# A gated scan and two feed-forward blocks: decay tiles of 129 columns per pair of heads, and three more chunks transposed by TensorE

## The chip, the cores and the metric

One Trainium2 chip, one of its cores. The metric is the device time of one execution in microseconds (us), smaller is better. Before the change the median of three executions is 585.96 us (584.48 to 587.40).

## What is computed

The reference has three stages. The first is a recurrence over time with a decay per key channel:

```
state = zeros((B, H, D, D))                       # B=4, H=8, S=768, D=48, fp32
for t in range(S):
    state = alpha[:, :, t, :, None] * state + einsum('bhd,bhe->bhde', k[:, :, t], v[:, :, t])
    y[:, :, t] = einsum('bhd,bhde->bhe', q[:, :, t], state)
```

`alpha` is drawn from 0.8 to 1.0. The heads of `y` are laid side by side to `x` of 4 x 768 x 384, and two feed-forward blocks follow: one with token mixing (`xk = mu_k*x + (1-mu_k)*x_prev`, `xr` likewise), `relu(xk @ w_k)**2 @ w_v` gated by `sigmoid(xr @ w_r)`; and one with `h = relu(x @ w_in)`, a convolution of three taps in time, a sigmoid gate, and `(h * gate) @ w_out`. The model width is 384, the inner width 1024.

## The kernel before, in words

The recurrence is done in chunks of C = 128 steps: 6 chunks for each of the 4 sequences, 24 in all. Two heads share the 128 partitions of a tile ("a pair"), so four pairs lie side by side in the free dimension. For each chunk three functions run:

- `prep(c)` (line 672) loads alpha, k, q and v, brings alpha, k and q from rows (time on the partitions) to columns (channel on the partitions), and makes the decays. `bt` is a product of the decays that runs backwards from the end of a pair, `gt` one that runs forwards; each is one `tensor_tensor_scan` over all four pairs at once. `kd = k*bt` and `qd = q*gt` are what the matmuls take, and `tt` holds, for each channel, the product over the whole chunk.
- `attend(c)` (line 717) scales the state `ss` by `tt`, forms the scores from `qd` and `kd` within the chunk (masked into `am`), and adds the chunk's keys and values to `ss`.
- `advance(c)` (line 763) makes the chunk's output from `am`, `vt`, `qd` and the kept states `ub`, and writes it into `xt`.

There are 12 units of T = 256 steps. A unit runs `mix` and `split`, `stage_k`, `stage_r`, `stage_v` (first block), `stage_h` and `stage_o` (second block). Products of two fp32 values are made as three matmuls of a high and a low part (`mm`, line 819); in the first two units some weights are still whole fp32 (`early_k`, `wvw`, `wrw`). While a unit runs, the two chunks of the next one are attended and the two after that prepared (`prep(c0 + 2)` in the loop at line 1074, `prep(n + 2)` in `att`, line 1046).

Two ways of transposing exist in `prep`, chosen by `by_pe = c < NPE`, with NPE = 5:

- By TensorE (chunks 0 to 4): rows are loaded with one DMA per tensor (`load(..., rows=True)`, line 651, runs of one head's 48 values), `turned` (line 685) takes a PSUM bank of the pool `banks` (line `turns`, at most two at a time) and transposes the four pairs against `ident`. Alpha is then copied by ScalarE out of PSUM; k and q are read by VectorE from PSUM in the very multiplication that makes `kd` and `qd`.
- By VectorE (chunks 5 to 23): four DMAs per tensor, already spread so that 32x32 block transposes suffice (lines 655 to 660), then one `transpose` (STREAM_TRANSPOSE in the profile) each for alpha, k and q, and the multiplications from SBUF.

The decays themselves, lines 691 to 704 of before:

```
raw = tmp_a.take(pl)                                # alpha lands here, one tile of the five of pool tmps
for x, cs in ((tc_, 0), (v3(adc)[:, :, 1:], slice(1, C))):
    pl.vector.tensor_scalar(x, v3(raw)[:, :, cs], LOW, HIGH, op0=ALU.max, op1=ALU.min)
pl.scalar.activation(raw, raw, AF.Abs, bias=-MID)   # these two count values outside 0.75 .. 1.25
pl.scalar.activation(raw, raw, AF.Relu, bias=-HALF, accum_out=odd[:, c:c + 1])
pl.vector.tensor_tensor_scan(v2(bt)[:, ::-1], ad[:, 1:NP * C + 1][:, ::-1], one_l[:, ::-1], 0.0, ...)
```

So alpha is clipped to 0.75 .. 1.25 in two pieces: the first step of each pair (4 columns) into `tc_`, a tile of `tt`; the other 127 steps of each pair (508 columns) into `ad`, whose first column per pair stays zero and ends the running product there. After the first scan `tc_` is multiplied by `bt`'s first column to give the whole product. If any value was out of range, `step_by_step` computes everything again after the main part; here none is.

`ad`, `bt`, `gt`, `rec_f` and `one_l` exist once; `qd`, `kd`, `tt` and `vt` exist twice; the tiles that take the loaded rows or blocks, `sa`, `sk`, `sq`, exist once (chunks 1 and 2 use spare tiles instead).

The order of the work is set by a planner at build time. All operations are recorded (`note`), each with a modelled cost (`cost`), and `issue` (line 277 of `Plan`) makes a list schedule for the five engines: at each step the engine that can start first takes the ready operation with the longest way to the end (`forward`, `pick`), then the ways are computed again from the end (`backward`); of six rounds the one with the shortest modelled end is written out. Every recorded instruction therefore carries line 297 in the profile, and is told apart by its tiles. A wait on an engine holds up everything behind it in that order. All DMAs go through SyncE's queue; GpSimd does a few memsets and small copies. In the first 30 us of its model the planner fills idle time of TensorE with matmuls that compute nothing (line 1095).

Of the kernel before, what the change touches and what calls it, by code (L numbers as in the profile page):

```python
# [11 lines left out]
F32 = mybir.dt.float32  # L12
# [3 lines left out]
AF = mybir.ActivationFunctionType  # L16
ALU = mybir.AluOpType
# [4 lines left out]
LOW, HIGH = 0.75, 1.25  # L22
MID, HALF = (HIGH + LOW) / 2, (HIGH - LOW) / 2
# [419 lines left out]
def gated_scan_ffn_kernel(  # L443
# [16 lines left out]
    nc = tc.nc  # L460
# [3 lines left out]
    P = 128  # L464
    C = 128
    HC = C // 2
    NP = H // 2
    ND = DM // P
    NF = DFF // P
# [5 lines left out]
    N4 = C // 32  # L475
    NRAW = 2
    NLENT = 12
    NPE = 5
    RAW = 768
    NTMP = 5  # L480
    NTEMP = 3
# [4 lines left out]
    ap = ctx.enter_context(tc.tile_pool(name="ap", bufs=1))  # L486
    fp = ctx.enter_context(tc.tile_pool(name="fp", bufs=1))
    pp = ctx.enter_context(tc.tile_pool(name="pp", bufs=1, space=PSUM))
    pl = Plan(nc)
# [5 lines left out]
    def fill(where, n):  # L495

        where.tile([P, n // 4], F32, name=f"fill{len(fills)}")
        fills.append(n)

    fills = []  # L500
    v3 = lambda x: x.rearrange("p (a b) -> p a b", b=C)
    v2 = lambda x: x.rearrange("p a b -> p (a b)")
    cols = lambda x, n: x.rearrange("p (a b) -> p a b", b=n)

    fill(fp, 160)
    tmps = pool(NTMP, fp, [P, 512], F32, "tmp")
    tmp_a, tmp_f = Line(tmps, 1), Line(tmps, 4)
    raws = Line(pool(NRAW, fp, [P, 2 * RAW], I32, "raw"))
# [12 lines left out]
    ident = cp.tile([P, P], F32, name="ident")  # L521
    mask = cp.tile([P, HC], U8, name="mask")
    mu_ks = cp.tile([P, ND], F32, name="mu_ks")
# [21 lines left out]
    sk = ap.tile([P, NP, N4 * D], F32, name="sk")  # L545
    sa = ap.tile([P, NP, N4 * D], F32, name="sa")
    vt = [ap.tile([P, NP, P], F32, name=f"vt{i}") for i in range(2)]
    ad = ap.tile([P, NP * C + 1], F32, name="ad")
    one_l = ap.tile([P, NP * C], F32, name="one_l")
    rec_f = ap.tile([P, NP * C], F32, name="rec_f")  # L550
    bt = ap.tile([P, NP, C], F32, name="bt")
    gt = ap.tile([P, NP, C], F32, name="gt")
    qd = [ap.tile([P, NP, C], F32, name=f"qd{i}") for i in range(2)]
    kd = [ap.tile([P, NP, C], F32, name=f"kd{i}") for i in range(2)]
    kbt = ap.tile([P, NP, P], F32, name="kbt")
# [106 lines left out]
    def blocks_in(s):  # L662
        return s.rearrange("p a (n d) -> p a n d", n=N4)[:, :, :, 0:32]

    def blocks_out(d):
        return d.rearrange("p a (t n) -> p a n t", n=N4)
# [5 lines left out]
    def prep(c):  # L672
        by_pe = c < NPE
        ia, ik, iq = early[c] if c in early else (sa, sk, sq)
        if c == NPE:

            for x, fill in ((sa, 1.0), (sk, 0.0), (sq, 0.0)):
                for r in (32, 96):
                    pl.gpsimd.memset(x[r:r + 32, :, N4 * D - 32:N4 * D - 16], fill)
        for x, y in ((alpha, ia), (k, ik), (q, iq), (v, vt[c % 2])):  # L680
            load(x, y, c // CPB, (c % CPB) * C, by_pe)
        adc = ad[:, 0:NP * C]
        qc, kc, tc_ = qd[c % 2], kd[c % 2], tt[c % 2]

        def turned(src):
            ps = turns.take(pl)
            for p in range(NP):
                pl.tensor.transpose(ps[:, p * C:(p + 1) * C], v2(src)[:, p * C:(p + 1) * C], ident)
            return ps

        raw = tmp_a.take(pl)
        if by_pe:
            pl.scalar.activation(raw, turned(ia), AF.Copy)
        else:
            pl.vector.transpose(blocks_out(v3(raw)), blocks_in(ia))
        for x, cs in ((tc_, 0), (v3(adc)[:, :, 1:], slice(1, C))):
            pl.vector.tensor_scalar(x, v3(raw)[:, :, cs], LOW, HIGH, op0=ALU.max, op1=ALU.min)
        pl.scalar.activation(raw, raw, AF.Abs, bias=-MID)
        pl.scalar.activation(raw, raw, AF.Relu, bias=-HALF, accum_out=odd[:, c:c + 1])
        pl.vector.tensor_tensor_scan(v2(bt)[:, ::-1], ad[:, 1:NP * C + 1][:, ::-1],  # L700
                                     one_l[:, ::-1], 0.0, op0=ALU.mult, op1=ALU.add)
        pl.vector.reciprocal(v3(rec_f)[:, :, 0], bt[:, :, 0])
        pl.vector.tensor_tensor(tc_, tc_, bt[:, :, 0], op=ALU.mult)
        pl.vector.tensor_tensor_scan(v2(gt), adc, rec_f, 0.0, op0=ALU.mult, op1=ALU.add)
        for x, y, z in ((kc, ik, bt), (qc, iq, gt)):
            if by_pe:
                pl.vector.tensor_tensor(x, v3(turned(y)), z, op=ALU.mult)
                continue
            pl.vector.transpose(blocks_out(x), blocks_in(y))
            pl.vector.tensor_tensor(x, x, z, op=ALU.mult)  # L710
# [290 lines left out]
    with tc.manual_schedule():  # L1001
        nc.vector.memset(ones, 1.0)
        make_identity(nc, ident)
        for y, eng in (((sa, sk, sq), nc.vector), *((x, pl.gpsimd) for x in early.values())):
            for x, fill in zip(y, (1.0, 0.0, 0.0)):
                eng.memset(cols(v2(x), 64)[:, 0:H, D:], fill)
        nc.vector.memset(ad, 0.0)
        nc.vector.memset(odd, 0.0)
        for x in kks.pool.tiles:
            nc.vector.memset(x[:, 0:NP * D], 0.0)  # L1010
        nc.vector.memset(least_s, least)
        nc.scalar.activation(odd1, ones[:, 0:1], AF.Sigmoid)
        for x in vt:
            nc.gpsimd.memset(x[:, :, D:80], 0.0)
        nc.gpsimd.memset(one_l, 0.0)
        nc.gpsimd.memset(v3(one_l)[:, :, C - 1:C], 1.0)
        nc.gpsimd.memset(rec_f, 0.0)
        mf = tmps.tiles[0]
        make_upper_triangular(nc, mf[:, :P])
        for i in range(2):  # L1020
            h = slice(HC * i, HC * i + HC)
            nc.vector.tensor_copy(mask[h], mf[h, h])
        for x in (am, *ub):
            nc.gpsimd.memset(x, 0.0)

        cw_raw = cp.tile([P, 3, NF, 2], I32, name="cw_raw")
        prep(0)
        col = NCH
        lent = Line(Pool([v2(ht)[:, 0:2 * RAW].bitcast(I32)]))
        for x, whole in zip(weights, (None, wrw, wvw, None, None)):  # L1030
            for y in pieces(x[0]):
                i = col - NCH
                weight(*x, y, lent if i < NLENT and i % 3 == 2 else raws, col, whole)
                col += 1
        for r in lent.roots:
            pl.seen.setdefault(ht.tensor.name, []).extend((True, 0, 4, -1, o) for o in r.ops)
        for x, y, z in ((mu_ks, nu_ks, mu_k), (mu_rs, nu_rs, mu_r)):
            pl.sync.dma_start(x, z.rearrange("(a p) -> p a", p=P))
            pl.vector.tensor_scalar(y, x, -1.0, 1.0, op0=ALU.mult, op1=ALU.add)
        for i in range(3):  # L1040
            pl.sync.dma_start(cw_raw[:, i], conv_w[i].bitcast(I32).rearrange("(f p t) -> p f t", p=P, t=2))
        narrow(cw, cw_raw)

        prep(1)

        def att(n):

            attend(n)
            advance(n)
            if n + 2 < NCH:  # L1050
                prep(n + 2)

        def early_k():
            return stage_k(mix(mu_ks, nu_ks, True), True), stage_r(mix(mu_rs, nu_rs, False, True))

        att(0)
        att(1)
        y = early_k()
        att(2)
        att(3)  # L1060
        x0 = stage_v(*y, True)
        y = early_k()
        settle(*weights[1], wrw)
        att(4)
        x1 = stage_v(*y, True)
        settle(*weights[2], wvw)
        big = stage_h(0, x0)
        att(5)
        stage_o(0, big, 0, True)
        xk = mix(mu_ks, nu_ks)  # L1070
        big = stage_h(1, x1)
        xr = mix(mu_rs, nu_rs)
        stage_o(1, big, 0, True)
        for u in range(2, NU):
            c0 = 2 * u + 2
            more = u + 1 < NU
            big = stage_k(xk)
            g = stage_r(xr)
            if more:
                attend(c0)  # L1080
            x = stage_v(big, g)
            if more:
                advance(c0)
                if c0 + 2 < NCH:
                    prep(c0 + 2)
            big = stage_h(u, x)
            if more:
                att(c0 + 1)
                xk = mix(mu_ks, nu_ks)
                xr = mix(mu_rs, nu_rs)  # L1090
            else:
                stage_last(T * NU - 1)
            stage_o(u, big)
        in_range()
        warm = lambda x: nc.tensor.matmul(x[0:64, 0:64], ones, ones, start=True, stop=True)
        pl.issue(600.0, 6, banks.pool, 30e3, warm)

        tc.mark_branch_hint_location("odd", "LikelyTaken", [getattr(mybir.EngineType, e) for e in ("PE", "SP", "DVE", "Activation")])
        n_even = nc.values_load(odd_i, min_val=0, max_val=P)
# [35 lines left out]
```

## Time and profile before

| | |
|---|---|
| median of three executions | 585.96 us |
| the profiled execution: time, span | 586.33 us, 584.4 us |
| its mean granted TensorE clock | 0.981 of full speed |
| busy: TensorE, VectorE, ScalarE, GpSimd | 564.0, 496.4, 434.4, 13.8 us |
| transposes by TensorE (alpha, k, q): sets of four | 15 |
| transposes by VectorE (alpha, k, q) | 57 |

The span runs from the first to the last instruction; the time of the same execution lies 1.9 us above it. PE is TensorE's matmul, PEld its weight load, DVE is VectorE, ACT ScalarE, POOL GpSimd, SP SyncE. A row of a group reads: line, engine, operation, out<-in by tile names, partitions x elements, count | busy us, mean ns of one | idle time of the engine just before them and what ended it. In a timeline the columns are start, duration, engine, line, operation, tiles, count, and in brackets the idle time before it and its releaser. A row of windows gives the stretch, its length, then the busy time of each engine with its count of instructions, the granted clock, the share of the DMA engines and GB/s. The ends of matmuls are modelled, and consecutive ones overlap in the records, so a small gap on PE does not show as idle time.

### The profile page before, as it was taken

How to read it: one execution, taken by the hardware profiler on the slowest of the kernel's cores; microseconds unless marked ns; L12 is line 12 of the kernel's file. 1: busy time of each engine (PE TensorE's matmuls, PEld its weight loads, DVE VectorE, ACT ScalarE, POOL GpSimd, SP SyncE). 2: the span in 40 equal slices, each digit the busy share in tenths (PEclk: the TensorE clock that was granted, in tenths of full speed). 3: DMA queues.
4: the chain of work that ended last, by engine and by line, in shares of the span. 5: the costliest groups of instructions: out<-in, count | busy, mean ns of one | idle time of the engine just before them, and what ended most of it. 6: DMA issues, size and time to landing. Idle time of an engine off the chain costs nothing.

```text
span 584.4 us, 18578 instructions
## 1 busy us (share of the span) xinstructions
PE 564.0 (97%) x7762; PEld 529.5 (91%) x7762; DVE 496.4 (85%) x1044; ACT 434.4 (74%) x1035; POOL 13.8 (2%) x61
## 2 busy tenths in 40 slices
PE   8789999999899999999999999999999999999997
PEld 7678788999789998998999998998999998999994
DVE  7999999999999989789789879789789879358263
ACT  4799998997669678677678668668668668658563
POOL 3000000000000000000000001000000001000000
PEclk9689999999979999999999999999999999999999
DMA  9977955003432323223222222233232211000000
GB/s 179 238 168 234 247 158 177 16 28 103 110 80 73 95 66 85 58 66 92 51 65 73 68 68 65 71 73 72 66 71 64 53 43 29 16 1 16 15 1 32
DMA packets 87404, 47.99 MB, mean 82 GB/s; under 512 B 49170, under 2 KB 81810, under 8 KB 87314
## 3 DMA queue, kind: packets, MB, share of 16 engines
q1 hardware_dynamic: 87314, 46.74, 32.4%
q8 instruction: 62, 1.02, 0.8%
q14 instruction: 28, 0.23, 0.1%
HBM read 42.00 MB, written 4.72 MB: 80 GB/s over the span
## 4 chain that ended last, share of the span: by engine, by line
PE 64%; DVE 20%; ACT 9%; DMA 2%; issue 2%; SPq 1%; POOL 0%; DVEq 0%; ACTq 0%; POOLq 0%
PE pf L297 54%; PE sc L297 6%; DVE tmp L297 6%; DVE x L297 3%; PE kk L297 3%; ACT tmp L297 3%; DVE qd L297 2%; DVE gt L297 2%; ACT raw L297 2%; DVE bigl L297 1%; ACT ht L297 1%; SPq L297 1%; DMA sq<-in_q_dram 1%; DVE kd L297 1%; DMA raw<-in_moe_w_v_dram 1%
## 5 line engine op out<-in xcount | busy, mean ns | idle before, releaser
L297 DVE SCALAR_TENSOR_TENSOR tmp<-ht,cw,tmp 128x256 f32<-128x256 f32 x192 | 86.5, 478 | 4.7 <-ACT tmp L297 4.2
L297 PE MATMUL pf<-bigh,wv 128*128 128x256 f32 x336 | 88.9, 308 | 0.5 <-DVE kd L297 0.5
L297 ACT ACTIVATE tmp<-tmp 128x256 f32<-128x256 f32 (+1 forms) x144 | 69.2, 485 | 24.9 <-DVE tmp L297 11.4
L297 PE MATMUL pf<-xh,wih 128*128 128x256 f32 x288 | 82.1, 286 | 2.5 <-ACT xh L297 1.5
L297 PE MATMUL pf<-xl,wih 128*128 128x256 f32 x288 | 81.5, 283 | 1.7 <-DVE xl L297 1.7
L297 PE MATMUL pf<-xl,wkh 128*128 128x256 f32 x288 | 81.2, 284 | 0.5 <-DVE xl L297 0.5
L297 PE MATMUL pf<-xh,wkh 128*128 128x256 f32 x288 | 79.3, 282 | 2.0 <-ACT xh L297 1.6
L297 PE MATMUL pf<-xh,wil 128*128 128x256 f32 x288 | 81.2, 282 | 0.0
L297 PE MATMUL pf<-xh,wkl 128*128 128x256 f32 x288 | 80.3, 281 | 0.0
L297 PE MATMUL pf<-bigh,wvh 128*128 128x256 f32 x240 | 68.3, 285 | 0.0
L297 PE MATMUL pf<-bigl,wvh 128*128 128x256 f32 x240 | 66.8, 278 | 0.0
L297 PE MATMUL pf<-woh,bigh 128*128 128x384 f32 x192 | 66.5, 347 | 0.1
L297 PEld LDWEIGHTS pf<-bigh,wv 128*128 128x128 f32 x336 | 62.8, 188 | 3.3 <-DVE kd L297 0.9
L297 PE MATMUL pf<-woh,bigl 128*128 128x384 f32 x192 | 64.7, 346 | 0.3 <-DVE bigl L297 0.3
L297 PE MATMUL pf<-wol,bigh 128*128 128x384 f32 x192 | 64.4, 339 | 0.0
L297 ACT ACTIVATE pf<-pf 128x512 f32<-128x512 f32 x88 | 51.1, 583 | 12.2 <-PE pf L297 10.9
L297 PEld LDWEIGHTS pf<-xh,wih 128*128 128x128 f32 x288 | 55.3, 192 | 3.8 <-ACT xh L297 1.8
L297 PEld LDWEIGHTS pf<-xl,wih 128*128 128x128 f32 x288 | 55.5, 193 | 2.1 <-DVE xl L297 2.1
L297 PEld LDWEIGHTS pf<-xh,wkh 128*128 128x128 f32 x288 | 54.4, 191 | 2.6 <-ACT xh L297 2.0
L297 PEld LDWEIGHTS pf<-xl,wkh 128*128 128x128 f32 x288 | 55.0, 191 | 1.3 <-DVE xl L297 0.9
L297 PEld LDWEIGHTS pf<-xh,wil 128*128 128x128 f32 x288 | 55.7, 193 | 0.0
L297 PEld LDWEIGHTS pf<-xh,wkl 128*128 128x128 f32 x288 | 54.8, 190 | 0.0
(164 smaller groups left out, 1393.1 us busy)
## 6 DMA issues: line engine op xcount, KB each, us to landing
vt<-in_v_dram SPq DMA_DIRECT2D x48, 96.0 KB, 3.3
out_dram<-ot SPq DMA_DIRECT2D x23, 192.0 KB, 2.1
sa<-in_alpha_dram SPq DMA_DIRECT2D x38, 96.0 KB, 2.2
sk<-in_k_dram SPq DMA_DIRECT2D x38, 96.0 KB, 2.5
sq<-in_q_dram SPq DMA_DIRECT2D x38, 96.0 KB, 2.2
raw<-in_moe_w_out_dram SPq DMA_DIRECT2D x4, 768.0 KB, 4.4
sa<-in_alpha_dram SPq DMA_DIRECT2D x38, 80.0 KB, 2.1
sk<-in_k_dram SPq DMA_DIRECT2D x38, 80.0 KB, 2.5
```

What stands on the lines that cost most here:

```text
L297: getattr(getattr(self.nc, x.eng), fn)(*args, **kw)
```

## The change

The decay tiles get E = 129 columns per pair instead of 128. Column 0 of each pair in `ad` stays zero, and all 128 decays of the pair follow it, so `bt[:, :, 0]` comes out of the scan as the product over the whole chunk, and `bt[:, :, 1:]`, `gt[:, :, 1:]` are the columns that multiply k and q. Nothing is clipped: alpha is written straight into `ad` (by ScalarE's copy out of PSUM, or by VectorE's transpose), both clips and the small multiplication go, and ScalarE copies `bt`'s first columns into `tc_`. ScalarE's first check reads `ad` and writes the spare tile `raw`, its second works on `raw` as before. NPE rises from 5 to 8. The unused filler `fill` shrinks by the bytes that the wider tiles take.

```diff
+    E = C + 1
-    NPE = 5
+    NPE = 8
-    fill(fp, 160)
+    fill(fp, 32)
-    ad = ap.tile([P, NP * C + 1], F32, name="ad")
-    one_l = ap.tile([P, NP * C], F32, name="one_l")
-    rec_f = ap.tile([P, NP * C], F32, name="rec_f")
-    bt = ap.tile([P, NP, C], F32, name="bt")
-    gt = ap.tile([P, NP, C], F32, name="gt")
+    ad = ap.tile([P, NP * E + 1], F32, name="ad")
+    one_l = ap.tile([P, NP * E], F32, name="one_l")
+    rec_f = ap.tile([P, NP * E], F32, name="rec_f")
+    bt = ap.tile([P, NP, E], F32, name="bt")
+    gt = ap.tile([P, NP, E], F32, name="gt")
...
-        adc = ad[:, 0:NP * C]
+        adc = ad[:, 0:NP * E]
...
+        av = cols(adc, E)[:, :, 1:]
+        if by_pe:
+            pl.scalar.activation(av, v3(turned(ia)), AF.Copy)
+        else:
+            pl.vector.transpose(blocks_out(av), blocks_in(ia))
         raw = tmp_a.take(pl)
-        if by_pe:
-            pl.scalar.activation(raw, turned(ia), AF.Copy)
-        else:
-            pl.vector.transpose(blocks_out(v3(raw)), blocks_in(ia))
-        for x, cs in ((tc_, 0), (v3(adc)[:, :, 1:], slice(1, C))):
-            pl.vector.tensor_scalar(x, v3(raw)[:, :, cs], LOW, HIGH, op0=ALU.max, op1=ALU.min)
-        pl.scalar.activation(raw, raw, AF.Abs, bias=-MID)
+        pl.scalar.activation(v3(raw), av, AF.Abs, bias=-MID)
         pl.scalar.activation(raw, raw, AF.Relu, bias=-HALF, accum_out=odd[:, c:c + 1])
-        pl.vector.tensor_tensor_scan(v2(bt)[:, ::-1], ad[:, 1:NP * C + 1][:, ::-1],
+        pl.vector.tensor_tensor_scan(v2(bt)[:, ::-1], ad[:, 1:NP * E + 1][:, ::-1],
                                      one_l[:, ::-1], 0.0, op0=ALU.mult, op1=ALU.add)
-        pl.vector.reciprocal(v3(rec_f)[:, :, 0], bt[:, :, 0])
-        pl.vector.tensor_tensor(tc_, tc_, bt[:, :, 0], op=ALU.mult)
+        pl.vector.reciprocal(cols(rec_f, E)[:, :, 0], bt[:, :, 0])
+        pl.scalar.activation(tc_, bt[:, :, 0], AF.Copy)
         pl.vector.tensor_tensor_scan(v2(gt), adc, rec_f, 0.0, op0=ALU.mult, op1=ALU.add)
-        for x, y, z in ((kc, ik, bt), (qc, iq, gt)):
+        for x, y, z in ((kc, ik, bt[:, :, 1:]), (qc, iq, gt[:, :, 1:])):
...
-        nc.gpsimd.memset(v3(one_l)[:, :, C - 1:C], 1.0)
+        nc.gpsimd.memset(cols(one_l, E)[:, :, C:], 1.0)
```

## Rows read from the trace of the kernel before

**Rows 1.** The page: busy time of each engine over the whole span.

```profile
PE 564.0 (97%) x7762; PEld 529.5 (91%) x7762; DVE 496.4 (85%) x1044; ACT 434.4 (74%) x1035; POOL 13.8 (2%) x61
```

**Rows 2.** Windows: the span cut at places where the picture changes.

```profile
0.00:41.00 41.00, 33.33 (x549) 28.07 (x552) 35.81 (x75) 28.38 (x59) 4.66 (x23) 0.83 1.01 199
41.00:97.00 56.00, 54.20 (x765) 47.37 (x758) 55.27 (x105) 53.76 (x112) 1.41 (x7) 1.00 0.74 208
97.00:134.00 37.00, 36.59 (x400) 35.32 (x401) 36.94 (x87) 34.44 (x92) 0.11 (x1) 1.00 0.12 36
...
146.00:163.00 17.00, 13.13 (x237) 11.82 (x226) 16.97 (x32) 9.98 (x23) 0.00 (x0) 0.98 0.49 117
163.00:170.00 7.00, 7.00 (x36) 7.00 (x37) 6.29 (x12) 3.64 (x9) 0.00 (x0) 0.56 0.45 110
170.00:570.00 400.00, 397.76 (x5627) 381.72 (x5627) 327.99 (x705) 290.46 (x716) 7.58 (x30) 1.00 0.22 55
```

**Rows 3.** Timeline of PE, 157 to 163 us: the waits before `stage_h` of unit 2.

```profile
158.98 0.39 PE L297 MATMUL pf<-xh,wih 128*128 128x256 f32 x1 [0.91 <-ACT xh L297]
160.51 0.38 PE L297 MATMUL pf<-xl,wih 128*128 128x256 f32 x1 [1.14 <-DVE xl L297]
...
161.93 0.50 PE L297 MATMUL pf<-xh,wih 128*128 128x256 f32 x2 [0.57 <-ACT xh L297]
162.96 0.58 PE L297 MATMUL pf<-xl,wih 128*128 128x256 f32 x1 [0.52 <-DVE xl L297]
```

**Rows 4.** Timeline of DVE, the same stretch.

```profile
157.55 0.74 DVE L297 TENSOR_TENSOR pf<-pf,x 128x512 f32<-128x512 f32 x1
...
159.79 0.67 DVE L297 TENSOR_TENSOR xl<-pf,xh 128x512 fp32r<-128x512 f32 x1
...
162.50 0.40 DVE L297 TENSOR_TENSOR xl<-pf,xh 128x256 fp32r<-128x256 f32 x1
```

**Rows 5.** Windows: sum over seven stretches, one per unit, of 12 to 14 us each.

```profile
sum 89.00, PE 86.77 PEld 81.89 DVE 86.81 ACT 77.69 POOL 5.12; mean PE 12.39 PEld 11.70 DVE 12.40 ACT 11.10 POOL 0.73
```

**Rows 6.** Groups of DVE by form: what the change removes or widens in `prep`.

```profile
L297 DVE TENSOR_TENSOR_SCAN bt<-ad,one_l 128x512 f32<-128x512 f32 x24 | 29.3, 1219 | 0.1
...
L297 DVE STREAM_TRANSPOSE tmp<-sa 128x512 f32<-128x512 f32 x19 | 21.0, 1108 | 0.5 <-DMA sa<-in_alpha_dram 0.4
...
L297 DVE TENSOR_SCALAR ad<-tmp 128x508 f32<-128x508 f32 x24 | 10.0, 418 | 2.6 <-ACT tmp L297 2.4
...
L297 DVE TENSOR_SCALAR tt<-tmp 128x4 f32<-128x4 f32 x24 | 3.9, 160 | 0.3
...
L297 DVE TENSOR_TENSOR tt<-tt,bt 128x4 f32<-128x4 f32 x24 | 3.6, 151 | 0.2
```

**Rows 7.** Groups of ACT by form: the copy out of PSUM, and a tiny copy.

```profile
L297 ACT ACTIVATE tmp<-pf 128x512 f32<-128x512 f32 x5 | 3.0, 597 | 4.4 <-POOL xt L297 3.1 <-PE pf L297 1.3
...
L297 ACT ACTIVATE xt<-xt 128x3 f32<-128x3 f32 x8 | 1.6, 197 | 0.0
```

**Rows 8.** Timeline of PE, 51 to 53 us: two sets of four transposes.

```profile
51.88 0.60 PE L297 MATMUL pf<-ident,sa 128*128 128x128 f32 x4
52.32 0.60 PE L297 MATMUL pf<-ident,sk 128*128 128x128 f32 x4
```

**Rows 9.** DMA issues of alpha's tile: blocks and rows (KB each, us to landing).

```profile
sa<-in_alpha_dram SPq DMA_DIRECT2D x38, 96.0 KB, 2.2
...
sa<-in_alpha_dram SPq DMA_DIRECT2D x3, 192.0 KB, 6.3
```

**Rows 10.** Timeline of SP, 151 us: the four block loads of one tensor.

```profile
151.65 1.80 SPq L297 DMA_DIRECT2D sa<-in_alpha_dram  x4
```

**Rows 11.** Timeline of DVE, 335 to 346 us: alpha of the next chunk around a `gt` scan.

```profile
335.75 1.12 DVE L297 STREAM_TRANSPOSE tmp<-sa 128x512 f32<-128x512 f32 x1
...
343.87 1.22 DVE L297 TENSOR_TENSOR_SCAN gt<-ad,rec_f 128x512 f32<-128x512 f32 x1
...
345.39 0.42 DVE L297 TENSOR_SCALAR ad<-tmp 128x508 f32<-128x508 f32 x1
```

## The prediction, made before the change was run

> **What bounds the kernel now.** I read the page's busy times first. TensorE is busy for 564.0 us of 584.4, VectorE for 496.4, ScalarE for 434.4 [rows 1]. So most of the time is TensorE's, and the question is where TensorE waits. The windows show it [rows 2]. The reader should compare, in each row, PE's busy time with the length of the stretch. From 0 to 41 us it lacks 7.7 us and its mean clock is 0.83: weights and inputs are still arriving (DMA share 1.01). From 41 to 134 us it lacks only 1.8 + 0.4 = 2.2 us, though VectorE (92.2 of 93) and ScalarE (88.2 of 93) are almost full too. From 146 to 163 us it lacks 3.9 us of 17, while VectorE is full (16.97) and ScalarE is not (9.98). From 163 to 170 us it is busy throughout, but at a mean granted clock of 0.56, nearly the lower of its two levels (1.2 of 2.4 GHz), just after those waits. From 170 to 570 us it lacks 2.2 us of 400.
>
> The waits before 163 us have a name: the first matmuls of `stage_h` of unit 2 wait for xh and xl, four times, 0.91, 1.14, 0.57 and 0.52 us [rows 3]. The timeline of VectorE shows why these are late [rows 4]: `pf*g` and the two xl subtractions stand between pieces of the preparations of chunks 7 and 8, and the last xl starts at 162.50, 4.9 us after the first product. VectorE is behind there; nothing else stands still on it. In the later units TensorE waits where a unit's `stage_h` meets its `stage_o`: seven such stretches lack 89.0 - 86.8 = 2.2 us together, VectorE being 97% busy in them [rows 5]. So VectorE's work has a price in two places, around 150 us and, little, in the seven stretches. Elsewhere it runs beside TensorE.
>
> **The change, part by part.** *Clips and small product.* Per chunk VectorE loses 418 + 160 + 151 = 729 ns, and each of two scans gets 4 columns more, 1219/512*4 = 10 ns; 0.71 us a chunk, 17.0 us over 24 [rows 6]. For it ScalarE gets a copy of 128x4; its nearest row, 128x3, takes 197 ns [rows 7], so 4.7 us in all. ScalarE lacks 11.8 us of being full in the three rows between 41 and 163 us and over 100 us after 170 [rows 2], so I cost it at nothing on the path; without that cover, in 41 to 134 us, three to five such copies are up to 1 us. The copy waits for the first scan; queued behind it on ScalarE are whatever evacuations the planner put next, and `attend`'s scaling of `ss` waits for it now across engines instead of behind VectorE's own product. That scaling comes long after the scan in most units.
>
> *Chunks 5 to 7 by TensorE.* VectorE loses nine block transposes of 1.10 us, 9.9 us [rows 6]. ScalarE gets three copies of 597 ns, 1.8 us [rows 7]. The multiplications remain, now out of PSUM. TensorE gets 36 transposes; a set of four moves the next set's start by 52.32 - 51.88 = 0.44 us, so nine sets are 4.0 us [rows 8]. These chunks are prepared between 60 and 155 us, where TensorE has little free time, so I charge them in full: **+4.0 us**. The lower bound is 0, if all fall into waits; the upper 5.4, if each costs its recorded 0.60. They also take three PSUM banks a chunk from the four that the stages rotate through; the reader of each is a ScalarE copy or a VectorE product, both shorter than 0.7 us, so I add nothing beyond that upper bound.
>
> Loads: each of nine tensors comes with one DMA in place of four; 192 KB in one instead of four of up to 96 [rows 9]. One landed in 6.3 us in the crowded start, against 2.2 us for a block load. SyncE's queue spends 1.80 us on four issues [rows 10], so it gets some 1.3 us shorter per tensor, 12 us over nine, and nothing is queued behind more than before. GpSimd's six memsets of padding move from chunk 5 to chunk 8, behind chunk 7's transposes and ahead of chunk 8's loads. GpSimd is idle then; the loads have several us. Both I cost at nothing; if DMA cover failed, the price would be the 4 us between the two landings, once.
>
> *The middle, 134 to 170 us.* VectorE is relieved there of the transposes of chunks 6 and 7 (6.6 us) and the clips of 6, 7 and 8 (2.2 us): 8.8 us, against an xl that is 4.9 us late. Then xl should follow its products, and the waits of 3.9 us and the low clock after them, (1 - 0.56)*7.0 = 3.1 us, have lost their cause: 7.0 us at stake [rows 2]. Next in line are the latencies pf, xh, xl themselves, which the small matmuls of `advance` cover only in part; I leave 1 us: **-6.0 us**, between 0 and -7.0.
>
> *41 to 134 us.* VectorE loses about 5 us here (clips of chunks 4 and 5, three transposes of chunk 5), but TensorE lacked only 2.2 us, and ScalarE, with 4.8 us free, gets 1.2 us more (one copy of 0.6, three of 0.2). **-1.0 us**, between -2.2 and +1.2.
>
> *The start.* Four chunks' clips (2.9 us) stand on VectorE's chain, but the weights' arrival sets much of it. Also `ad` is now filled by ScalarE directly, so that the copy of chunk 1 has to wait for chunk 0's `gt` scan, which the spare tile had spared it. **-0.5 us**, between -2.9 and +0.5.
>
> *After 170 us.* 0.71 us less VectorE work for each chunk, but the wait is 2.2 us in all, and the spare tile is lost here too: in eight chunks alpha was transposed before the `gt` scan of the chunk before it (in the one shown at 335.75, scan at 343.87, clip at 345.39) [rows 11]. Now the transpose writes `ad` and must follow that scan, so 1.1 us of VectorE moves from a slack stretch into or behind a full one. The next `bt` scan is some 20 us away, so it can be put off. **-1.0 us**, between -2.2 and, if it is not put off, +5.4 (8 times 1.10 - 0.42).
>
> Sum: 4.0 - 6.0 - 1.0 - 0.5 - 1.0 = -4.5 us. The profiled execution took 586.33 us, 0.37 over the median of 585.96, so 581.8 becomes **581.4 us** on the median's scale.
>
> One rule speaks against the change. What the rows show: PEld 91% and PE 97% busy, DVE 85% [rows 1]. The Trainium skill, Perfetto Trace Analysis, "Identifying the Most-Contended Engine", says that improving a kernel means improving the engine with the highest occupancy, TensorE being judged by its weight loads; by that the change moves work to the wrong engine, and the sum would be +4.0 alone, 590.0 us, against 581.4 by the stretches. The same page's "Optimization Strategy" grants that regimes differ over time, and the windows of this trace do.
>
> **The rivals.** *The middle wait stays (slower).* The xl's lateness could be ended by something other than VectorE's backlog: by xh, on which two of the four waits end, or by chunk 8's block loads, which SyncE issues right there. TensorE then pays 4.0 us and gets nothing: 590.0 us. For it speaks that TensorE is full; against it that VectorE is at 16.97 of 17.0 and ScalarE waits for its product there. It decides as soon as the waits before unit 2's `stage_h` stay above 3 us. This is also where the page's rule would come out right. 0.17.
>
> *The lost spare tile.* All as forecast, but the planner puts alpha's transposes right behind the `gt` scans, in the full stretches: +5.4 in place of -1.0 is 587.8; half of them, 585.1. No change to be seen. For it: VectorE is 97% busy in those stretches. Against it: 20 us of freedom and a planner that looks for a short end. 0.15. With it I count ScalarE becoming the pace in 41 to 134 us together with only half the middle's gain: 4.0 - 3.0 + 1.2 - 0.5 - 1.0 = +0.7, 586.7 us, also no change. 0.10.
>
> *More gain.* With VectorE 27 us lighter the planner writes another order, and the start, which lacks 7.7 us and much clock, tightens too: the lower ends with half the transposes charged, 2.0 - 7.0 - 2.2 - 2.9 - 2.2 = -12.3, give 573.7 us. 0.12.
>
> That the change doesn't do what it says would show in counts only: no path is left by which a clip could stay.
>
> **How the numbers follow.** A measurement of this kernel can tell about 0.5% from no change, 2.9 us. The forecast, 577.5 to 585 us, has 0.46, the rest as above. It and the larger gain are below 583.0 except for some 0.04 of the forecast: faster 0.54. The two middle rivals and that 0.04 make 0.29 for the same. The slower rival has 0.17. The range, 574.0 to 590.0 us, runs from just above the larger gain to the slower rival; the halves of these two that lie beyond, and what I have not thought of, are the 0.2 left out.
>
> **What would show it.** Counts: 24 sets of transposes against `ident` of alpha, k and q on PE, 16 of each block transpose on DVE, no row ad<-tmp, 24 copies of 128x4 on ACT. Busy times: DVE 496.4 - 17.0 - 9.9 = 469.5 us, ACT 434.4 + 4.7 + 1.8 = 440.9. Step by step: the same chunks' preparations no longer fill VectorE around 150 us, PE's four waits are under 1 us together, and the granted clock stays at its upper level from 146 to 170 us (the middle); PE's idle time in seven stretches is below 2 us (after 170 us). Alpha's transpose between a `gt` scan and `stage_h`'s products would mean the lost spare tile. A low clock that merely moves to another place, or a `stage_h` of unit 2 that starts as late as before, would make the forecast wrong; so would sets of transposes that take over 0.6 us of TensorE each, or matmuls that wait for a bank.

## The result, and the profile after

The changed kernel takes 591.68 us (median of four executions, 590.21 to 593.12) against 586.34 us for the kernel before on the same chip: a ratio of 1.0095, 95% interval 1.0078 to 1.0111. It is slower, where 581.4 us and a gain were forecast, and it lies above the range of 574 to 590 us. The profiled execution took 590.21 us, span 588.4 us, mean granted clock 0.991.

The page's first row, busy time of each engine, answers to [rows 1]:

```profile
PE 561.3 (95%) x7800; PEld 525.3 (89%) x7800; DVE 476.4 (81%) x963; ACT 434.1 (74%) x1062; POOL 14.5 (2%) x61
```

Groups of DVE and of ACT, by form, answer to [rows 6, 7]. The clips and the small product are gone, 16 block transposes of alpha are left, and ScalarE has its 24 small copies:

```profile
L297 DVE TENSOR_TENSOR_SCAN bt<-ad,one_l 128x516 f32<-128x516 f32 x24 | 29.4, 1226 | 0.3 <-ACT ad L297 0.2
L297 DVE STREAM_TRANSPOSE ad<-sa 128x512 f32<-128x512 f32 x16 | 17.4, 1091 | 0.0
...
L297 ACT ACTIVATE tmp<-ad 128x512 f32<-128x512 f32 x24 | 15.2, 632 | 14.9 <-DVE ad L297 14.7
L297 ACT ACTIVATE tt<-bt 128x4 f32<-128x4 f32 x24 | 5.0, 206 | 9.3 <-DVE ss L297 5.8 <-DVE bt L297 3.1
```

So the change did what it says, and VectorE's busy time is 20 us shorter. The windows of the changed kernel, cut as in [rows 2], show what TensorE made of it:

```profile
0.00:41.00 41.00, 30.32 (x570) 25.85 (x570) 36.80 (x66) 29.64 (x64) 4.56 (x23) 0.92 1.03 201
41.00:97.00 56.00, 54.15 (x746) 47.42 (x745) 54.11 (x97) 54.99 (x118) 0.11 (x1) 1.00 0.80 212
97.00:134.00 37.00, 35.30 (x454) 33.40 (x453) 37.00 (x85) 36.46 (x92) 0.97 (x7) 1.00 0.19 47
...
146.00:163.00 17.00, 16.10 (x217) 15.60 (x216) 8.30 (x14) 8.31 (x21) 0.00 (x0) 1.00 0.20 49
163.00:170.00 7.00, 7.00 (x61) 7.00 (x61) 6.83 (x12) 4.91 (x14) 0.00 (x0) 1.00 0.55 123
170.00:570.00 400.00, 393.77 (x5594) 375.06 (x5594) 313.89 (x647) 283.92 (x716) 8.83 (x30) 1.00 0.22 55
```

Read each against its row of [rows 2]. From 146 to 170 us the gain came: TensorE lacks 0.9 us instead of 3.9, and the clock stays at its upper level. From 97 to 134 us it lacks 1.7 us instead of 0.4. From 170 to 570 us it lacks 6.2 us instead of 2.2, although VectorE is 14 us less busy there. The last row is most of the loss. The views of PE's waits, 185 to 545 us, give a name to 3.0 of these 4.0 us; first the kernel before, then the changed one (total us, times, longest):

```profile
PE kk L297 <- ACT kbt L297: 2.2, 5, 0.6
```

```profile
PE kk L297 <- ACT kbt L297: 5.2, 11, 0.8
```

The products of keys and values in `attend` (`kk<-vt,kbt`) wait for ScalarE's copy of `kbt` out of PSUM, eleven times instead of five. The timeline of DVE in one such unit of the changed kernel shows what stands ahead:

```profile
208.67 0.69 DVE L297 TENSOR_TENSOR qd<-qd,gt 128x512 f32<-128x512 f32 x1
209.40 1.24 DVE L297 TENSOR_TENSOR_SCAN gt<-ad,rec_f 128x516 f32<-128x516 f32 x1
210.55 0.46 DVE L297 SCALAR_TENSOR_TENSOR tmp<-ht,cw,tmp 128x256 f32<-128x256 f32 x1
210.93 1.08 DVE L297 STREAM_TRANSPOSE ad<-sa 128x512 f32<-128x512 f32 x1
211.87 1.31 DVE L297 SCALAR_TENSOR_TENSOR tmp<-ht,cw,tmp 128x256 f32<-128x256 f32 x3
```

And ACT, the same stretch:

```profile
210.78 0.39 ACT L297 ACTIVATE ht<-pf 128x256 f32<-128x256 f32 x1
212.05 0.64 ACT L297 ACTIVATE tmp<-ad 128x512 f32<-128x512 f32 x1 [0.88 <-DVE ad L297]
212.59 0.40 ACT L297 ACTIVATE tmp<-tmp 128x256 f32<-128x256 f32 x1
212.89 0.37 ACT L297 ACTIVATE ht<-pf 128x256 f32<-128x256 f32 x1
...
218.24 0.58 ACT L297 ACTIVATE kbt<-kk 128x512 f32<-128x512 f32 x1
218.72 0.62 ACT L297 ACTIVATE tmp<-tmp 128x512 f32<-128x512 f32 x1
```

Chunk 12's alpha is transposed at 210.93, right behind chunk 11's `gt` scan, amid the products of `stage_h`. Before, chunk 12's stood ahead of the products of `stage_h`, and the scan followed 7 us later:

```profile
203.92 1.13 DVE L297 STREAM_TRANSPOSE tmp<-sa 128x512 f32<-128x512 f32 x1
...
211.06 1.23 DVE L297 TENSOR_TENSOR_SCAN gt<-ad,rec_f 128x512 f32<-128x512 f32 x1
```

With alpha comes its range count: the first pass waits 0.88 us at the head of ScalarE's queue for the transpose and works 0.64 us ahead of the next `ht` copy out of PSUM; the second pass takes 0.62 us right behind the `kbt` copy that TensorE waits for, ahead of what `stage_o` needs next. The same order, a `gt` scan and 1.5 us later the next chunk's alpha, recurs at each even chunk from 12 to 22.

For this and the kernels of the experiments below the spans were cut at the start of the second `ot` copy of units 2 and 10 and of the last one (timeline of ACT, tile ot); the last column is the length of 170 to 570 us less PE's busy time there:

```
us                  to unit 2  units 3-10  last unit  behind it   span   PE idle 170-570
before                185.7      354.0       40.5        4.2     584.4      2.2
after                 184.4      358.5       39.9        5.7     588.4      6.2
e1_pe8_only           189.7      354.0       39.9        5.7     589.3      2.9
e2_decays_only        186.1      358.4       39.9        5.8     590.2      5.6
e3_two_ad             185.2      358.0       39.9        5.7     588.8      5.9
e4_spare_copy         187.6      354.8       39.9        5.7     588.0      2.9
e5_two_ad_early       184.3      353.4       39.8        5.7     583.1      2.3
e6_tt_on_dve          186.8      358.7       39.8        7.6     592.9      6.8
e7_no_checks          188.0      355.0       39.7        5.6     588.3      4.2
e8_alpha_late         184.2      354.2       39.8        5.6     583.8      2.9
e9_early_npe5         187.0      352.7       39.7        5.6     585.0      2.7
e10_check_late        184.6      356.1       39.7        5.6     586.0      4.5
```

The sum for the change: -1.3 to the end of unit 2, +4.5 in units 3 to 10, -0.7 in the last unit, +1.5 behind the last copy. The last is a single execution of before against all others, e1_pe8_only with its old decays among them; whether before always ends so quickly was not tried.

### The profile page after: what moved, and what is told of

It is laid out like the page before. It is cut to its first block, busy times and chain, and to the rows that moved or that the text cites. A ratio compares the mean times of both kernels' runs of the same rounds, so it can differ in the third digit from the quotient of the medians.

```text
span 588.4 us, 18547 instructions
## 1 busy us (share of the span) xinstructions
PE 561.3 (95%) x7800; PEld 525.3 (89%) x7800; DVE 476.4 (81%) x963; ACT 434.1 (74%) x1062; POOL 14.5 (2%) x61
## 4 chain that ended last, share of the span: by engine, by line
PE 41%; DVE 35%; ACT 17%; issue 3%; DMA 2%; POOL 0%; DVEq 0%; ACTq 0%
PE pf L297 33%; DVE tmp L297 9%; DVE x L297 6%; ACT tmp L297 5%; PE sc L297 4%; DVE qd L297 4%; ACT pf L297 3%; DVE bigl L297 3%; DVE ad L297 3%; DVE bt L297 2%; PE kk L297 2%; ACT bigh L297 2%; DVE gt L297 2%; DVE xl L297 2%; DVE kd L297 2%
## 5 line engine op out<-in xcount | busy, mean ns | idle before, releaser
L297 PE MATMUL pf<-xl,wih 128*128 128x256 f32 x288 | 80.0, 278 | 0.0
L297 PE MATMUL pf<-xh,wil 128*128 128x256 f32 x288 | 80.0, 278 | 0.0
L297 ACT ACTIVATE tmp<-tmp 128x256 f32<-128x256 f32 (+1 forms) x120 | 53.6, 454 | 8.1 <-DVE tmp L297 7.3
L297 PEld LDWEIGHTS pf<-xh,wih 128*128 128x128 f32 x288 | 54.1, 188 | 3.0 <-DVE kd L297 1.1
L297 DVE TENSOR_TENSOR bigl<-pf,bigh 128x512 fp32r<-128x512 f32 x40 | 27.3, 683 | 35.4 <-ACT bigh L297 35.4
L297 PEld LDWEIGHTS pf<-xh,wil 128*128 128x128 f32 x288 | 54.4, 189 | 0.0
```

What stands on the lines that cost most here:

```text
L297: getattr(getattr(self.nc, x.eng), fn)(*args, **kw)
```

## The experiments

Every ratio is to the kernel before, run beside it on the same chip; kernels are compared with each other through it, and stage by stage through the table, which has one execution of each.

**The two parts alone.** First only the three chunks on TensorE:

```diff
-    NPE = 5
+    NPE = 8
```

> The kernel before with NPE = 8 alone (clips, spare tile and product kept). Theory (the loss after 170 us comes from alpha going straight into the one ad tile): nothing of that loss, so the middle's gain of about 6 us against 4.0 us of transposes: 1 to 4 us faster than before, 582 to 585.5 us. Rival (the three chunks on TensorE are what costs): 590 us or more.

Measured: 591.08 us, ratio 1.0058 (1.0033 to 1.0083): slower, where a gain was expected, and where the rival had put it. Units 3 to 10 lose nothing, as expected, but the end of unit 2 comes 4.0 us later. The middle gives only part of its gain, as the windows below show, and new waits come before it: from 41 to 134 us TensorE lacks 5.1 us, where it lacked 2.2, and the granted clock from 41 to 97 us is 0.97. The longest of these waits stands ahead of a set of transposes:

```profile
58.88 0.66 PE L297 MATMUL pf<-ident,sa 128*128 128x128 f32 x4 [1.77 <-DVE kd L297]
```

Then only the decays, the changed kernel with `NPE = 5`:

> The changed kernel with NPE = 5, so the decay tiles alone. Theory: the loss of 4 to 5 us after 170 us is all here, and VectorE is 17 us lighter, of which the middle takes 1 to 3 us: 588 to 591 us, slower than before. Rival (transposes are what costs): 584 us or less.

Measured: 591.69 us, ratio 1.0066 (1.0043 to 1.0089), 0.7 us above what was expected. In the table the +4.5 of units 3 to 10 is whole in the second and absent in the first: it belongs to the decays. Ahead of unit 3 the parts don't add: alone they end it at 189.7 and 186.1, together at 184.4. The windows of the middle show much of why, first of e1_pe8_only:

```profile
146.00:163.00 17.00, 14.99 (x124) 14.57 (x124) 16.30 (x30) 10.72 (x24) 0.00 (x0) 0.97 0.44 104
163.00:170.00 7.00, 7.00 (x53) 7.00 (x53) 2.14 (x4) 0.93 (x2) 0.00 (x0) 0.83 0.21 52
```

and of e2_decays_only:

```profile
146.00:163.00 17.00, 15.66 (x262) 14.70 (x260) 16.90 (x27) 11.16 (x27) 0.00 (x0) 1.00 0.50 119
163.00:170.00 7.00, 6.43 (x41) 6.30 (x42) 6.48 (x11) 3.85 (x10) 0.00 (x0) 0.76 0.48 105
```

Idle time plus what the clock withheld, (1 - granted) times 7.0: of the 7.0 us of before, e1 keeps 2.0 + 1.2 = 3.2 and e2 keeps 1.3 + 0.6 + 1.7 = 3.6; both together keep 0.9. VectorE is still full in each (16.30, 16.90 of 17) and only half full (8.30) in the changed kernel.

**Is it ScalarE's small copy?** The copy of 128x4 goes back to VectorE:

```diff
-        pl.scalar.activation(tc_, bt[:, :, 0], AF.Copy)
+        pl.vector.tensor_copy(tc_, bt[:, :, 0])
```

> The changed kernel with the small copy into tt on VectorE instead of ScalarE (128x4, about 0.15 us each). Theory: within 1.5 us of the changed kernel, since alpha's transposes stay where they are. Rival (ScalarE's copy): 3 us or more faster than the changed kernel.

Measured: 593.53 us, ratio 1.0110 (1.0084 to 1.0136) against 1.0095 for the changed kernel. Units 3 to 10 stay at 358.7. The copy is not the cause.

**Is it the range count?** Both of ScalarE's passes are left out, so this kernel doesn't look for values out of range:

```diff
-        raw = tmp_a.take(pl)
-        pl.scalar.activation(v3(raw), av, AF.Abs, bias=-MID)
-        pl.scalar.activation(raw, raw, AF.Relu, bias=-HALF, accum_out=odd[:, c:c + 1])
```

> The changed kernel without the two ScalarE operations per chunk that count alphas out of range (that part of the computation is left out). They free ad late and stand in the stage_h stretch too. Theory: about half of the loss after 180 us is theirs (1.5 us of ScalarE per chunk in the stretch, against 1.1 us of VectorE): 1.5 to 4 us faster than the changed kernel. Rival (ScalarE's small copy): up to 1.5 us faster, as ScalarE is relieved in general.

Measured: 589.80 us, ratio 1.0035 (1.0017 to 1.0052). Units 3 to 10 are 355.0, so 3.5 of the 4.5 us go with 24 x (0.63 + 0.62) us of ScalarE's work, while alpha stays in the stretch (its transpose starts 1.5 us after the `gt` scan here too). But work was taken away in all stretches, so this alone does not say that the place matters.

**The spare tile back.** Alpha lands in the spare tile again, and one copy of 128x512 by VectorE brings it to `ad`:

```diff
+        raw = tmp_a.take(pl)
...
-            pl.vector.transpose(blocks_out(av), blocks_in(ia))
+            pl.vector.transpose(blocks_out(v3(raw)), blocks_in(ia))
+        pl.vector.tensor_copy(av, v3(raw))
```

> The changed kernel, alpha again into the spare tile and from there by one VectorE copy of 128x512 into ad; the product still comes out of the scan. Theory: the loss after 170 us goes as with two tiles, against 24 copies of 0.4 us on VectorE: 585.5 to 589 us. Rival (ScalarE's small copy): within 1.5 us of the changed kernel.

Measured: 589.26 us, ratio 1.0030 (1.0019 to 1.0042), 0.3 us above what was expected. Units 3 to 10 fall to 354.8: with the spare tile 3.7 of the 4.5 us are gone. Chunk 12's transpose stands 16 us ahead of chunk 11's `gt` scan now, and the copy follows that scan, as the clip did before. The range count follows the copy, so it is still in the stretch, in this unit (timeline of ACT) and at each even chunk from 12 to 22:

```profile
214.55 0.63 ACT L297 ACTIVATE tmp<-tmp 128x512 f32<-128x512 f32 x1 [0.70 <-DVE ad L297]
...
220.88 0.62 ACT L297 ACTIVATE tmp<-tmp 128x512 f32<-128x512 f32 x1
```

In exchange VectorE makes 24 copies of 419 ns, and the front, where it is full, ends later (187.6).

**A second `ad` in place of the copy.** Odd chunks from 8 on take a piece of a tile that is unused by then:

```diff
+    ad_b = raws.pool.tiles[1][:, 0:NP * E + 1].bitcast(F32)
...
+        ad = ad_b if c >= 8 and c % 2 else ad_a
```

> The changed kernel with a second ad tile for the odd chunks from the ninth on (in a weight buffer that is free by then), so that a chunk's alpha need not wait for the gt scan of the chunk before. Theory: the loss after 170 us goes, 4 to 5 us faster than the changed kernel, 586 to 588 us, and alpha's transposes lie again ahead of the gt scans. Rival (ScalarE's new small copy and its wait for the scan delay the copies that TensorE waits for): within 1.5 us of the changed kernel.

Measured: 590.43 us, ratio 1.0051 (1.0032 to 1.0071): the expectation failed. Units 3 to 10 stay at 358.0. DVE's timeline says why (`raw` is the second tile):

```profile
210.05 1.23 DVE L297 TENSOR_TENSOR_SCAN gt<-raw,rec_f 128x516 f32<-128x516 f32 x1
...
211.58 1.09 DVE L297 STREAM_TRANSPOSE raw<-sa 128x512 f32<-128x512 f32 x1
```

The planner used the freedom to run alpha one chunk further ahead, and chunk 13's now follows the scan of chunk 11, which frees that same tile, in the same stretch. A buffer more is no cure while nothing says where the work should stand.

**Two tiles, and an order.** As above, and each alpha from chunk 10 on is tied to the `bt` scan of the chunk before:

```diff
+            if c > 9:
+                pl.ops[-1].deps.add(mark[c - 1])     # alpha's transpose
...
+        mark[c] = pl.ops[-1]                         # the bt scan
```

> Two ad tiles as in the run before, and the planner is also told that a chunk's alpha transpose (from the eleventh chunk on) comes after the first scan of the chunk before, so that alpha no longer runs a further chunk ahead; it then lies in VectorE's slack ahead of the gt scan, as in the kernel before. Theory (alpha's transpose and its ScalarE check inside the stage_h stretch cost 4 us after 170 us): TensorE's lost time after 180 us falls by 3 to 4.5 us, 585.5 to 588.5 us. Rival (ScalarE's small copy for tt): within 1.5 us of the changed kernel.

Measured: 585.04 us against 586.69 us, ratio 0.9968 (0.9954 to 0.9983): a little faster than the kernel before. DVE in the same unit, then PE's waits and the long window of this kernel:

```profile
199.14 1.22 DVE L297 TENSOR_TENSOR_SCAN bt<-raw,one_l 128x516 f32<-128x516 f32 x1
...
200.74 1.08 DVE L297 STREAM_TRANSPOSE ad<-sa 128x512 f32<-128x512 f32 x1
```

```profile
PE kk L297 <- ACT kbt L297: 2.1, 5, 0.4
```

```profile
170.00:570.00 400.00, 397.70 (x5643) 379.45 (x5645) 317.85 (x663) 287.62 (x722) 7.64 (x30) 1.00 0.22 54
```

**One tile, same operations, another place.** The changed kernel; alpha of even chunks from 10 on waits for the k product of the chunk before, some 20 us later:

```diff
+            if c > 9 and c % 2 == 0:
+                pl.ops[-1].deps.add(mark[c - 1])     # alpha's transpose
...
+            mark.setdefault(c, pl.ops[-1])           # the product kd*bt
```

> The changed kernel, one ad tile, the same operations; the planner is only told that alpha's transpose of the even chunks from the eleventh on waits for the kd product of the chunk before, which moves it out of the stage_h stretch to behind the mixing. Theory: the loss after 180 us goes but for 1 us, 586.5 to 589 us. Rival (ScalarE's small copy): within 1.5 us of the changed kernel.

Measured: 586.67 us, ratio 0.9995 (0.9980 to 1.0009). Chunk 12's alpha at its new place, PE's waits and the long window:

```profile
231.65 1.08 DVE L297 STREAM_TRANSPOSE ad<-sa 128x512 f32<-128x512 f32 x1
```

```profile
PE kk L297 <- ACT kbt L297: 2.6, 6, 0.5
```

```profile
170.00:570.00 400.00, 397.15 (x5630) 379.17 (x5632) 319.47 (x663) 285.86 (x725) 8.02 (x30) 1.00 0.23 55
```

No operation was added, taken away or resized, and 4.3 of the 4.5 us of units 3 to 10 came back. One such dependency lets the planner arrange other operations anew too, so this run alone does not isolate the place. The table does: whatever else the planner did, the four kernels with an alpha's transpose and its count amid the products of `stage_h` (after, e2, e3, e6) take 358.0 to 358.7 us in units 3 to 10, and the six with the transpose elsewhere (before, e1, e4, e5, e8, e9) 352.7 to 354.8. The place of alpha, with what hangs on it, is the cause. It could indeed "be put off" at next to no cost (354.2 against 354.0 before); the planner only didn't do it.

**Transpose or count?** Now alpha stays in the stretch, and only its range count is held back, by the same two lines behind its first pass instead of the transpose:

```diff
         pl.scalar.activation(v3(raw), av, AF.Abs, bias=-MID)
+        if c > 9 and c % 2 == 0:
+            pl.ops[-1].deps.add(mark[c - 1])
```

> The changed kernel with alpha's transpose left where the planner puts it (behind the gt scan of the chunk before, in the full stretch), and only ScalarE's range count (two passes over 128x512) of the even chunks from 10 on held back until the k product of the chunk before, some 20 us later. Theory A (VectorE's 1.1 us in the stretch is the cost): units 3 to 10 stay near 358 us, ratio to before about 1.008. Theory B (ScalarE's two passes of 1.28 us, which follow alpha into the stretch and delay the evacuations there, are the cost; leaving the count out gave back 3.4 of 4.5 us): units 3 to 10 about 355, ratio about 1.002.

Measured: 588.13 us, ratio 1.0027 (1.0015 to 1.0040). Between the two: units 3 to 10 are 356.1. Moving the count alone gives back 358.5 - 356.1 = 2.4 of the 4.3 us, and moving the transpose as well another 356.1 - 354.2 = 1.9. The other order is in e4_spare_copy, where the count is in the stretch and the transpose is not: 354.8. Against e8_alpha_late, which has neither there, the count (with its copy of 0.42 us on VectorE) costs 354.8 - 354.2 = 0.6, the transpose 1.9, and both 4.3: together more than their sum, so the loss can't be divided between them. Why they add up to more was not tried. PE's waits, and ACT's first pass at its new place:

```profile
PE kk L297 <- ACT kbt L297: 3.7, 8, 0.7
```

```profile
230.33 0.62 ACT L297 ACTIVATE tmp<-ad 128x512 f32<-128x512 f32 x1
```

**What the three chunks on TensorE are worth once the stretch is repaired.** The two-tile kernel with an order, and `NPE = 5`:

> The two-tile kernel that orders alpha early (e5_two_ad_early), with chunks 5 to 7 transposed by VectorE again (NPE = 5). Theory: the decays alone left the front (to the end of unit 2's stage_o) at 186.1 us and the decays with the three chunks on TensorE at 184.3, so here front about 186, units 3 to 10 about 353.5, end 45.4: span about 585, time about 587, ratio to before about 1.000; the three chunks on TensorE are then worth about 2 us, not their price of 4. Rival: with the stretch repaired, TensorE's 36 extra transposes are a pure cost of 3 to 4 us: front about 181, time about 582, ratio about 0.991.

Measured: 587.52 us, ratio 1.0009 (0.9987 to 1.0032), against 0.9968 (0.9954 to 0.9983) with the three chunks on TensorE. The rival, a pure cost of 3 to 4 us, falls: without them the time is 2.4 us longer by the ratios, and the front ends 2.7 us later. One of the places, PE's timeline and the window behind it:

```profile
71.33 0.39 PE L297 MATMUL pf<-xh,wkh 128*128 128x256 f32 x1 [2.75 <-ACT xh L297]
```

```profile
71.70:75.20 3.50, 3.30 (x16) 3.25 (x16) 3.50 (x10) 2.75 (x6) 0.00 (x0) 0.51 0.56 118
```

TensorE waits 2.75 us and then runs 3.5 us at its lower level (0.51), which costs another 1.7 us; the same pair, a wait of 2.23 us and 3.4 us at 0.50, stands at 102.5 us. e5_two_ad_early, with `NPE = 8`, has neither.

## Why the prediction was wrong

**The step that failed** is in "After 170 us": "The next `bt` scan is some 20 us away, so it can be put off. -1.0 us". It measured +4.5 in units 3 to 10. The rival "The lost spare tile" had the event right, down to the sign that was named for it (alpha between a `gt` scan and `stage_h`'s products), and nearly its size, +5.4; it was given 0.15, and its total of 587.8 us fell short by the terms below. What spoke against it, 20 us of freedom, was freedom for a planner that orders by its own modelled costs. e8_alpha_late shows that the freedom existed, e3_two_ad that the planner fills more of it in the same way. With alpha placed ahead of the scans the term itself comes out: units 3 to 10 take 353.4 and 352.7 us in e5 and e9, where 354.0 - 1.0 was forecast.

**Its price, 8 x (1.10 - 0.42),** counted VectorE alone. e4_spare_copy measures this very exchange, 0.42 us behind the scan in place of the transpose, at 358.5 - 354.8 = 3.7 us; six alphas came to stand there (chunks 12 to 22), and 6 x 0.68 is 4.1. The size is right, but in part by luck: moving alpha moves what follows it, two passes of 0.63 and 0.62 us on ScalarE, and with these out of the way (e10_check_late) the same six transposes cost 1.9 us, not 4. [Rows 5] have VectorE 97% busy in the seven stretches; the same row has ACT at 77.69 of 89.00, 87%, and the wait that grew ends on ScalarE. The loss also isn't spread evenly: against e8_alpha_late the changed kernel loses 1.3, 1.3, 1.1 and 0.8 us in units 3, 4, 6 and 7 and nothing in 5 and 8, though alpha stands at the same place there. Those two attend the first chunk of a sequence, which has no state to scale and keeps one copy less; that this is the reason wasn't tried.

**The middle, -6.0**, was right: idle time from 3.9 to 0.9 us in 146 to 163 us and the 3.1 us of the clock behind it, -6.1. Both parts of the change were needed for it, as e1 and e2 show, though not in proportion to the relief: 6.6 us of it (e1) and 2.2 us (e2) each left about half of the 7.0. One reading was off: what stands between the rows shown in [rows 4] is all chunk 8's work, not 7's and 8's. Chunk 8's alpha, first before and then in the changed kernel:

```profile
156.61 1.09 DVE L297 STREAM_TRANSPOSE tmp<-sa 128x512 f32<-128x512 f32 x1
```

```profile
142.23 1.09 DVE L297 STREAM_TRANSPOSE ad<-sa 128x512 f32<-128x512 f32 x1
```

It now stands ahead of the stretch, and VectorE is busy for 8.7 us less in 146 to 163 us: the relief acted by letting VectorE's work run ahead.

**Nine sets of transposes, +4.0**, was right as TensorE's work. Two sets of the changed kernel, timeline of PE, with the waits that came to this stretch:

```profile
58.38 0.63 PE L297 MATMUL pf<-ident,sa 128*128 128x128 f32 x4 [0.74 <-DMA sa<-in_alpha_dram]
...
60.59 0.66 PE L297 MATMUL pf<-ident,sk 128*128 128x128 f32 x4
61.09 0.60 PE L297 MATMUL pf<-ident,sq 128*128 128x128 f32 x4
61.52 0.81 PE L297 MATMUL pf<-bigh,wv 128*128 128x256 f32 x3
...
121.67 0.38 PE L297 MATMUL pf<-xh,wih 128*128 128x256 f32 x1 [0.64 <-ACT ot L297]
...
129.73 0.38 PE L297 MATMUL pf<-xh,wih 128*128 128x256 f32 x1 [0.95 <-DVE kd L297]
```

They advance by 61.09 - 60.59 = 0.50 and 61.52 - 61.09 = 0.43 us, against 0.44 in [rows 8]. Summed over a kernel, with every advance of PE (from one start to the next) cut off at its shape's median over all twelve kernels so that waits drop out, TensorE's work is 476.3 and 480.0 us in e2 and the changed kernel, 476.0 and 480.6 in e9 and e5: 3.7 and 4.6 us more with the nine sets.

**41 to 134 us, -1.0**, was mis-sized, beyond its bound of +1.2: idle time rose from 2.2 to 1.9 + 1.7 = 3.6 us. Of the three waits above, two belong to things costed at nothing. Chunk 5's rows landed 5.7 us after their issue, 0.74 us late for TensorE (the price of 4 us "once" was a bound for that). And the bank that chunk 7's k was transposed into was still being read by the `kd` product when `stage_h`'s first matmul needed it: 0.95 us, the "matmuls that wait for a bank" that were named as a sign. The 0.64 is a bank held by ScalarE's `ot` copy, ScalarE being 36.46 of 37 us busy.

**The start, -0.5**, can't be read directly, since clock and idle time both moved (0.83 and 7.7 us lacking in [rows 2], 0.92 and 10.7 here). What is left of -1.3 after +1.4 (41 to 134), -6.1 and +3.7 to +4.6 is -0.3 to -1.2: the size forecast, but only by difference.

**ScalarE's small copy at nothing** held: 206 ns each, and e6_tt_on_dve gained nothing by moving it to VectorE. **The busy times** announced, DVE 469.5 and ACT 440.9, came out as 476.4 and 434.1. The durations, added up over the trace, did change as worked out (DVE by -26.7, ACT by +6.8 us), but the page's busy time counts overlapping records once, and records do overlap (DVE's add up to 569.7 us before, against 496.4 busy); sums of durations don't subtract from it.

**The rule** of the Trainium skill, Perfetto Trace Analysis, "Identifying the Most-Contended Engine", would have given 590.0 us, nearer to 591.7 than the forecast. The runs are divided on it. e1_pe8_only bears it out: the nine sets alone, added to the busiest engine, ended unit 2 4.0 us later. Between e9 and e5 the same sets gained 2 us. For the changed kernel it gives nearly the right number by the wrong way: the middle wait, which the rival tied to it takes to stay, went, and what was lost was lost on VectorE and ScalarE, in units where TensorE had been given no work.

From the forecast to the result, then: 4.5 + 1.0 = 5.5 us in units 3 to 10, 1.4 + 1.0 = 2.4 between 41 and 134 us and 1.5 behind the last copy, less 0.7 in the last unit, make 8.7; the spans differ by 588.4 - (584.4 - 4.5) = 8.5 us. The profiled execution was the shortest of four; the median is 1.5 us above it.

## What to carry to other kernels

Removing a copy also removes the buffer that let its producer run early: ask where the producer will stand now, list everything that hangs on it on all engines, and price that place by the stretch it falls into. Where a planner orders the work, freedom to put something off is no reason that it will be; if the place matters, tie it down with a dependency, which here was worth 4.3 us with no other edit. And two reliefs of one full engine may each give about half and only together end its wait, as 3.2 and 3.6 of 7.0 us were left here and then 0.9, so parts measured alone need not add up.

## What was not expected of the hardware

In e9_early_npe5 a wait of TensorE of 2.75 us and one of 2.23 us were each followed at once by some 3.5 us at the lower level (0.51 and 0.50), so that each cost another 1.7 us beyond its own length. The kernel before shows a like stretch from 163 us on, after its four waits, [rows 2, 3]; the changed kernel has no such stretch between 41 us and its last 4 us.
